# Second weights of a part row tile: a transfer from HBM in place of eight GpSimd sums per job

## The chip, the cores and the metric

One core of one Trainium2 chip runs the whole program. The metric is the device time of one execution in microseconds (us), the median of the timed runs. The engines are called TensorE (PE, its weight loads PEld), VectorE (DVE), ScalarE (ACT), GpSimd (POOL) and SyncE (SP; in this kernel it only issues transfers). A measurement of this kernel tells about 0.2% from no change.

## What is computed

The reference runs a linear attention over 3072 tokens and then two layers of experts. In the second layer each token goes to one of 8 experts, and this is what the change touches:

```python
expert_idx = np.argmax(logits, axis=1)
...
for e in range(E):
    mask = expert_idx == e
    ...
    xe = x[mask]
    h = np.maximum(xe @ w1[e], 0.0)
    ye = h @ w2[e]
    out[mask] = gate_w[mask, None] * ye
```

A token has 384 features, the hidden layer has 1024, all in float32.

## The kernel before

The attention fills the first part of the span. Then the experts follow one another as *jobs*: a job is one expert on a fixed number of token slots. The first layer's jobs and the first two of the second layer have 256 slots or fewer; then come seven jobs of the second layer with 448, 448, 448, 416, 416, 384 and 384 slots. The first five of these seven have a part of a row tile (64 or 32 rows beside three full tiles of 128) and are called J1 to J5 in the text. The experts of the last six jobs are known only at run time; their numbers sit in registers of SP.

A job on 448 slots has 24 *slots of work*. In slots 0 to 7 `gemm1` makes one block of the hidden layer each: nine products on PE into a bank of PSUM, of which three are in turn (`g1`, `bufs=3`). The float32 weights and activations are split into a high and a low part, which the fast product takes (`w1h`, `w1l`, `w2h`, `w2l`, `xh`, `xl`, `hh`, `hl`). A bank is read by ACT (`hh`, line 1040), then by DVE (`hl`, line 1041), then, for the part tile's columns, by ACT again (`hr`, line 1044); after that PE may fill it anew. In slots 8 to 23 `gemm2` makes the second product, four slots for each row tile. The part tile is the third (slots 16 to 19); it doesn't use the split but plain float32: `hr` times `w2r` (line 1060). Its second weights `w2r`, 128 x 8 x 384 values in one buffer, are rebuilt on POOL as the sum of the high and the low part, one block in each of the slots 0 to 7 (line 1045).

Beside that, `work` does in each slot what the other engines owe to the next jobs, in an order fixed by hand. Six pieces of the next job's weights are split in slots 0, 4, 8, 12, 16 and 20 (`conv_w`): ACT copies the high part (line 859), DVE or, for pieces 2 and 5, POOL subtracts it (line 860), and SP then loads the piece of the job after the next into the free staging buffer (`load_w`, lines 840 and 842). In slot 2 SP loads the next job's rows (`load_rows`, lines 1005 and 1007). In slots 9, 13 and 15 PE transposes them (line 1017). Finished rows are scattered to the output by POOL (line 273). SP issues its transfers in program order and waits at each until its buffer is free.

The buffers `w2r` and `hr` lie in the pool `f3`, which takes the place of a pool of the jobs before J1.

Of the kernel before, what the change touches and what calls it, by code (L numbers as in the profile page):

```python
# [24 lines left out]
E = 8  # L25
# [17 lines left out]
POOL_LO = (2, 5)  # L43
# slots of a job at which a piece of the next weights is split, and blocks of the next rows are transposed, by the job's row tiles
CONV = {
# [7 lines left out]
W_LO, W_HI = 0.25, 1.5  # L53
# row tiles that are gated together, by their first: how many, and after how many slots
GROUPS = {0: (4, 2), 4: (4, 2), 8: (4, 2), 12: (4, 2), 16: (4, 0), 20: (3, 1), 23: (1, 1)}
# [9 lines left out]
def general(tc, t, out, ident, rev, wg):  # L65
    """The whole computation for any values: the recurrence token by token, each expert on all tokens."""
    nc = tc.nc
# [117 lines left out]
def attn_moe_moe_kernel(ctx: ExitStack, tc: tile.TileContext, t, out):  # L185
# [15 lines left out]

# [1 line left out]
    ident = const.tile([128, 128], F32, name="ident")  # L203
# [52 lines left out]
    def prefill(buf, a, b):  # L256
        """empty slots, in blocks of 128"""
        nc.sync.dma_start(
            out=buf[a * 128:b * 128].rearrange("(a p) c -> p a c", p=128),
            in_=zrow.unsqueeze(1).to_broadcast([128, b - a, ROW]))  # L260

# [1 line left out]
    rt_p = fctx.enter_context(tc.tile_pool(name="rt", bufs=2))  # L263

    def logits_T(lt_ps, xT, n):
        """gate logits of n rows from their transpose: a part of the sum on each quarter of the partitions"""
        for kb in range(KB):
            T.matmul(lt_ps[32 * kb:32 * kb + 32], lhsT=wg[:, kb, :], rhs=xT[:, kb, 0:n], start=True, stop=True)
# [13 lines left out]
    def route(lt, X, g0, n, two, idx_out, ec):  # L282
        """lt: [96, n * 128] parts of the logits; X: row tiles; ec: which first slots.  Yields the engine of the operation to come."""
        sets = 2 if two else 1
# [67 lines left out]

# [1 line left out]
    gens = []  # L354
# [4 lines left out]
    def start(g, lag=0, burst=False, mult=1):  # L359
        """one at a time: they share a bank and the counts"""  # L360
        if gens:
            queue.append((g, lag, burst, mult))
        else:
            gens.append([g, next(g), slot[0] + lag, mult, burst])

    def tick(kind, now=False, burst=False):
        """the next operation of the gating under way if it waits for this engine; after another engine's, some slots later"""
        for x in gens[:]:
            if x[1][:3] == kind[:3] and (now or slot[0] >= x[2]):
                while True:  # L370
                    x[1] = next(x[0], None)
                    if x[1] is None:
                        gens.remove(x)
                        if queue:
                            start(*queue.pop(0))
                    elif kind != "pe " and x[4] and x[1][:3] in ("dve", "act"):
                        continue
                    elif x[1][:3] == kind[:3]:
                        if burst and kind != "pe ":
                            continue  # L380
                    else:
                        x[2] = slot[0] + x[3] * (int(x[1][3:]) if x[1][3:].strip() else 1)
                    return
# [19 lines left out]

# [1 line left out]
    def attention():  # L405
        with ExitStack() as actx:
# [54 lines left out]
            def gap(eng, x, r0):  # L461
                """rows r0..r0+31 of x become zero (those below the gap are written later)"""
                if eng is A:
                    A.copy(out=x[r0:r0 + 32], in_=warm_src[r0:r0 + 32, 0:x.free_size()])
                else:
                    eng.memset(x[r0:r0 + 32], 0.0)
# [11 lines left out]
            def check_w():  # L478
                """powers of w out of range: counted with the slots that overflow"""
                w2 = cst.tile([112, H], F32, name="w2")  # L480
                okw = cst.tile([112, H], F32, name="okw")
                w_ = w_c.rearrange("p h o -> p (h o)")
                V.tensor_tensor(out=w2, in0=w_, in1=w_, op=ALU.mult)
                V.tensor_scalar(out=okw, in0=w2, scalar1=W_LO, scalar2=None, op0=ALU.is_ge)
                V.tensor_scalar(out=w2, in0=w2, scalar1=W_HI, scalar2=None, op0=ALU.is_le)
                V.tensor_tensor(out=okw, in0=okw, in1=w2, op=ALU.mult)
                V.tensor_reduce(out=w2[:, 0:1], in_=okw, axis=AX.X, op=ALU.min)
                V.tensor_scalar(out=cum[0:112, 16:17], in0=w2[:, 0:1], scalar1=0.5, scalar2=None, op0=ALU.is_lt)
# [61 lines left out]
            def prep_kq(n):  # L550
                """keys for the states, and the values times what each token gives to its own output"""
                hb, j = n // LT, n % LT
# [17 lines left out]
            def amat(n):  # L570
# [6 lines left out]
                for X, r0 in ((XE[x], 0), (XO[x], 64)):  # L577
                    A.copy(out=fl(X[r0:r0 + 64]), in_=fl(a_ps[r0:r0 + 64]))
                # keys before the query; below partition 64 all of the odd buffer stays
                for X, n_, base in ((XE[x], 64, 0), (XO[x], 128, 64)):  # L580
# [4 lines left out]
            def uy(nu, uodd, ny, yodd):  # L585
                """state products of chunk (nu, uodd) between the output products of (ny, yodd)"""
                if nu is not None:
# [64 lines left out]
            def gate_route(lt, g0, gn):  # L652
# [3 lines left out]
                for c, k, end in ((0, 17, EARLY), (8, 18, NT)):  # L656
                    if g0 + gn == end:
                        # from here the first expert's slots are counted anew
                        yield "dve"
# [57 lines left out]
            for n in range(NT):  # L717
                # TensorE: state of the even half, outputs of the previous odd half
                uy(n, 0, n - 1 if n else None, 1)
# [85 lines left out]

# [1 line left out]
    W1 = [t["w1a"], t["w1b"]]  # L807
# [7 lines left out]
    def expert(n):  # L815
        """of the last ones, the one whose count comes at this place"""
        if n not in regs:
# [4 lines left out]
    def load_w(n, j):  # L822
        """piece j of six of the n-th expert's weights"""
        if n >= 2 * E:
# [5 lines left out]
        if n == 1:  # L830
            # the next but one's place, free until its own come
            if j == 0:
# [12 lines left out]
    def conv_w(n, j):  # L845
        """the piece as a sum of two that the fast float32 product takes exactly"""
        if n >= 2 * E:
# [48 lines left out]

# [1 line left out]
    rows0 = first.tile([128, 2, ROW], F32, name="rows0")  # L898
# [9 lines left out]
    def first_T(tp, kbs, a, b):  # L908
        """columns a..b of the transpose; of a row tile all, so that no part of it starts within"""
        a0 = a - a % 128  # L910
# [69 lines left out]

# [1 line left out]
    jobs = [(0, n, n * CAP1, CAP1) for n in range(E)] + [(1, E, 0, CAPS), (1, E, CAPS, CAPS)]  # L982
# [5 lines left out]
    def tiles_of(cap):  # L988
        """row tiles; a part of one comes between"""
        nf, half = divmod(cap, 128)  # L990
        t = [(i, 128) for i in range(nf)]
        if half:
            t.insert(2, (nf, half))
        return t
# [28 lines left out]
    def gemm1(j, fb):  # L1023
# [6 lines left out]
        if fb == 0:  # L1030
            ps = (first, pools["rows"]) if j <= LAST_S else (pools["h"],) * 2
            extra = []
            if cap > full:
                extra = [pools["h"].tile([128, FB, x], F32, tag=t, bufs=1, name=t) for t, x in (("w2r", DM), ("hr", cap - full))]
            hT[j] = [p.tile([128, FB, full], F32R, tag=t, bufs=1, name=t) for p, t in zip(ps, ("hh", "hl"))] + extra
        hh, hl = hT[j][0:2]
# [5 lines left out]
        if cap > full:  # L1042
            w2, hr = hT[j][2:4]
            A.activation(out=hr[:, fb], in_=p[:, full:cap], func=ACTF.Relu)  # L1044
            P.tensor_tensor(out=w2[:, fb], in0=wts[n][2][:, fb].bitcast(F32), in1=wts[n][3][:, fb].bitcast(F32), op=ALU.add)

    def gemm2(j, k, i, m, q):
        """two of the blocks of the second product; a part of a tile takes them in plain float32 on the parts of the columns"""
        l, n, base, cap = jobs[j]
# [50 lines left out]
    def work(j, k):  # L1100
        """what slot k of job j has for the other engines"""
        slot[0] += 1
# [41 lines left out]
    def by_count(tot):  # L1144
        """the last experts' places by their counts, and whether every expert and place has slots enough"""
        over = ids_p.tile([1, 19], F32, tag="over", name="over")
# [100 lines left out]
```

## Time and profile before

| What | Value |
|---|---|
| median of 3 timed runs | 642.01 us (641.26 to 642.4) |
| the profiled execution, its span from the first to the last instruction | 648.0 us |
| of the span: PE busy | 562.8 us (87%) |
| DVE busy | 405.8 us (63%) |
| ACT busy | 295.4 us (46%) |
| POOL busy | 298.7 us (46%) |
| transfers, mean over the span | 162 GB/s |

The times of single instructions come from the profiled execution, whose time is its span; it was 6.0 us longer than the median of the timed runs. Shares are averages over stages with different limits; what a change of one stage is worth is read from the waits in that stage.

### The profile page before, as it was taken

The page shows a single profiled execution, that of the slowest core. Times are in us where ns is not written, and L with a number is a line of the kernel's source. Part 1 is how long each engine was busy: PE and PEld are TensorE (multiplying, and loading weights), DVE is VectorE, ACT ScalarE, POOL GpSimd, SP SyncE. Part 2 cuts the span into 40 slices and gives each one's busy share as a digit, 9 for nine tenths or more (in the row PEclk, how much of TensorE's full clock was granted, in tenths as well). Part 3 has the DMA queues.
Part 4 walks back from the last instruction along what each step waited for, and adds up shares of the span by engine and source line. Part 5 has one row for each costly group of instructions (what it writes and reads, how often), then busy time and mean ns, then how long its engine had stood idle before and what let it go on. Part 6 is the DMA issues. An engine that isn't in the chain of part 4 may idle for free. (4 is left out here: it accounts for less than half of the span.)

```text
span 648.0 us, 13115 instructions
## 1 busy us (share of the span) xinstructions
PE 562.8 (87%) x5186; PEld 501.0 (77%) x5188; DVE 405.8 (63%) x732; ACT 295.4 (46%) x584; POOL 298.7 (46%) x312
## 2 busy tenths in 40 slices
PE   5796678778789989999999999997979979699993
PEld 3585566666667888898988999986869868599993
DVE  7998999999725467756676535436454464655320
ACT  5664455564425545554455426443424334254320
POOL 7765585776623175655323224644272524523201
PEclk8877888887979999999999999997998989799997
DMA  8985988679162987676665436342323434333000
GB/s 184 241 203 151 280 213 216 154 171 351 56 220 83 303 277 226 203 243 189 197 183 167 149 105 193 127 148 98 126 79 122 154 105 131 104 127 109 35 13 26
DMA packets 51896, 104.69 MB, mean 162 GB/s; under 512 B 5724, under 2 KB 37592, under 8 KB 51824
## 3 DMA queue, kind: packets, MB, share of 16 engines
q1 hardware_dynamic: 44016, 89.15, 47.7%
q0 software_dynamic: 5904, 11.82, 5.0%
q10 hardware_dynamic: 1904, 2.78, 1.7%
q8 instruction: 43, 0.70, 0.5%
q14 instruction: 29, 0.24, 0.1%
HBM read 82.98 MB, written 26.96 MB: 170 GB/s over the span
## 5 line engine op out<-in xcount | busy, mean ns | idle before, releaser
L1039 PE MATMUL g<-xh,w1h 128*128 128x256 f32 (+3 forms) x384 | 126.4, 329 | 19.1 <-ACT hr L1044 19.1
L1039 PE MATMUL g<-xh,w1l 128*128 128x256 f32 (+3 forms) x384 | 122.8, 320 | 0.0
L1039 PE MATMUL g<-xl,w1h 128*128 128x256 f32 (+3 forms) x384 | 122.4, 319 | 0.0
L1041 DVE SCALAR_TENSOR_TENSOR hl<-g,hh 128x256 fp32r<-128x256 f32 (+1 forms) x128 | 61.2, 480 | 93.1 <-ACT hh L1040 92.5
L1063 PE MATMUL g<-w2h,hh 128*128 128x384 f32 x312 | 109.2, 350 | 0.0
L1063 PE MATMUL g<-w2h,hl 128*128 128x384 f32 x312 | 105.5, 338 | 0.0
L1063 PE MATMUL g<-w2l,hh 128*128 128x384 f32 x312 | 105.2, 337 | 0.0
L1039 PEld LDWEIGHTS g<-xh,w1h 128*128 128x128 f32 x384 | 74.4, 194 | 25.4 <-ACT hr L1044 20.5
L1040 ACT ACTIVATE hh<-g 128x256 fp32r<-128x256 f32 (+1 forms) x128 | 55.1, 430 | 70.1 <-PE g L1039 68.8
L860 POOL TENSOR_TENSOR w1l<-s,w1h 128x1024 fp32r<-128x1024 f32 x14 | 33.4, 2389 | 114.1 <-ACT w1h L859 69.0
L1039 PEld LDWEIGHTS g<-xl,w1h 128*128 128x128 f32 x384 | 74.4, 194 | 1.8 <-DVE xl L1021 0.2
L1039 PEld LDWEIGHTS g<-xh,w1l 128*128 128x128 f32 x384 | 74.2, 193 | 1.6
L860 DVE TENSOR_TENSOR w1l<-s,w1h 128x1024 fp32r<-128x1024 f32 x28 | 57.6, 2056 | 20.9 <-ACT w1h L859 20.9
L273 POOL DMA_INDIRECT xs<-xall,idx_all x48 | 52.3, 1089 | 38.0 <-DVE cum L351 15.9
L273 POOL DMA_INDIRECT out<-rows,ids x30 | 29.2, 973 | 87.3 <-ACT rows L894 62.4
L1063 PEld LDWEIGHTS g<-w2h,hh 128*128 128x128 f32 x312 | 59.3, 190 | 3.1 <-issue 3.0
L1021 DVE TENSOR_TENSOR xl<-xt_ps,xh 128x256 fp32r<-128x256 f32 (+3 forms) x48 | 23.7, 495 | 57.3 <-ACT xh L1020 53.4
L1063 PEld LDWEIGHTS g<-w2l,hh 128*128 128x128 f32 x312 | 58.9, 189 | 0.1
L1063 PEld LDWEIGHTS g<-w2h,hl 128*128 128x128 f32 x312 | 58.5, 188 | 0.0
L606 PE MATMUL yp<-VSE,XE 112*64 112x48 f32 x384 | 31.5, 243 | 26.7 <-DVE xall L617 25.2
L606 PEld LDWEIGHTS yp<-VSE,XE 112*64 112x64 f32 x384 | 28.3, 157 | 28.6 <-DVE xall L617 26.9
L860 DVE TENSOR_TENSOR w2l<-s,w2h 128x1152 fp32r<-128x1152 f32 x28 | 37.9, 1354 | 14.0 <-ACT w2h L859 13.5
(194 smaller groups left out, 1207.2 us busy)
## 6 DMA issues: line engine op xcount, KB each, us to landing
s<-in_w1b SPq DMA_DIRECT2D x24, 512.0 KB
s<-in_w1a SPq DMA_DIRECT2D x21, 512.0 KB
RK<-in_rk SPq DMA_DIRECT2D x24, 384.0 KB
kr<-in_kr SPq DMA_DIRECT2D x12, 768.0 KB
s<-in_w2b SPq DMA_DIRECT2D x16, 576.0 KB
s<-in_w2a SPq DMA_DIRECT2D x14, 576.0 KB
xs<-zrow SPq DMA_DIRECT2D x5, 970.0 KB
VSE<-in_v SPq DMA_DIRECT2D x12, 384.0 KB
```

Of the source, the lines that this page charges most:

```text
L273: i = P.indirect_dma_start(out=dst, out_offset=bass.IndirectOffsetOnAxis(ap=idx_col, axis=0), in_=src, in_offset=None, bounds_check=last, ...
L606: T.matmul(y_ps[ny][0:64, h, 0:D], lhsT=XE[x][0:112, h], rhs=VSE[iy][0:112, jy, h], start=True, stop=True)
L860: (P if j in POOL_LO else V).tensor_tensor(out=lo, in0=x, in1=hi.bitcast(F32), op=ALU.subtract)
L1021: V.tensor_tensor(out=lo, in0=tp[:, 0:cap], in1=hi.bitcast(F32), op=ALU.subtract)
L1039: T.matmul(p, lhsT=a[:, kb, f], rhs=b[:, kb], start=(kb == 0 and i == 0), stop=(kb == KB - 1 and i == 2))
L1040: A.activation(out=hh[:, fb], in_=p[:, 0:full], func=ACTF.Relu)
L1041: V.scalar_tensor_tensor(out=hl[:, fb], in0=p[:, 0:full], scalar=0.0, in1=hh[:, fb].bitcast(F32), op0=ALU.max, op1=ALU.subtract)
L1063: T.matmul(p, lhsT=a[:, fb, r], rhs=b[:, fb], start=(fb == 0 and x == 0), stop=(fb == FB - 1 and x == 2))
```

## The change

In a job with a part tile the eight sums on POOL are gone. Instead one transfer on SP's queue brings the expert's second weights (1.57 MB) from HBM straight into `w2r`, issued where the buffers of the job's hidden layer are taken, ahead of the first slot's work. The product of the part tile stays as it is. The rest of the diff are comments and empty lines.

```diff
             if cap > full:
                 extra = [pools["h"].tile([128, FB, x], F32, tag=t, bufs=1, name=t) for t, x in (("w2r", DM), ("hr", cap - full))]
+
+                e = expert(n) if base is None else n - E
+                nc.sync.dma_start(out=extra[0], in_=W2[l][ds(e, 1)].rearrange("o (f p) d -> p (o f) d", p=128))
             hT[j] = [p.tile([128, FB, full], F32R, tag=t, bufs=1, name=t) for p, t in zip(ps, ("hh", "hl"))] + extra
...
         if cap > full:
-            w2, hr = hT[j][2:4]
+            hr = hT[j][3]
             A.activation(out=hr[:, fb], in_=p[:, full:cap], func=ACTF.Relu)
-            P.tensor_tensor(out=w2[:, fb], in0=wts[n][2][:, fb].bitcast(F32), in1=wts[n][3][:, fb].bitcast(F32), op=ALU.add)
```

## Rows read from the trace of the kernel before

**Rows 1.** The page's first line.
```profile
span 648.0 us, 13115 instructions
```

**Rows 2.** Waits of PE, 400 to 648 us: us in total, times, longest.
```profile
PE g L1039 <- ACT hr L1044: 19.1, 4, 6.2
```

**Rows 3.** Timeline of ACT, DVE, POOL, start of J2: start us, us, engine, line.
```profile
446.25 0.22 ACT L1044 ACTIVATE hr<-g 128x64 f32<-128x64 f32 x1 [6.63 <-DVE hl L1041]
...
439.26 6.49 DVE L860 TENSOR_TENSOR w1l<-s,w1h 128x1024 fp32r<-128x1024 f32 x1 [1.23 <-ACT w1h L859]
445.68 0.54 DVE L1041 SCALAR_TENSOR_TENSOR hl<-g,hh 128x384 fp32r<-128x384 f32 x1
...
436.91 7.75 POOL L1045 TENSOR_TENSOR w2r<-w2h,w2l 128x384 f32<-128x384 f32 x8
```

**Rows 4.** Timeline of DVE and POOL, start of J4 and of J5.
```profile
516.68 6.67 DVE L860 TENSOR_TENSOR w1l<-s,w1h 128x1024 fp32r<-128x1024 f32 x1 [1.20 <-ACT w1h L859]
...
514.52 7.75 POOL L1045 TENSOR_TENSOR w2r<-w2h,w2l 128x384 f32<-128x384 f32 x8
...
553.05 8.15 DVE L860 TENSOR_TENSOR w1l<-s,w1h 128x1024 fp32r<-128x1024 f32 x1 [1.20 <-ACT w1h L859]
...
552.42 7.70 POOL L1045 TENSOR_TENSOR w2r<-w2h,w2l 128x384 f32<-128x384 f32 x8
```

**Rows 5.** Timeline of DVE and POOL in J1.
```profile
406.70 1.22 DVE L860 TENSOR_TENSOR w1l<-s,w1h 128x1024 fp32r<-128x1024 f32 x1 [1.23 <-ACT w1h L859]
...
414.14 1.58 DVE L860 TENSOR_TENSOR w1l<-s,w1h 128x1024 fp32r<-128x1024 f32 x1 [1.23 <-ACT w1h L859]
...
407.62 8.99 POOL L1045 TENSOR_TENSOR w2r<-w2h,w2l 128x384 f32<-128x384 f32 x8 [3.23 <-issue]
```

**Rows 6.** Line 1045, all instructions: ns min/median/max, first and last start, forms.
```profile
L1045 POOL TENSOR_TENSOR w2r<-w2h,w2l x40: 980/1013/2031, 407.6 to 559.1; 128x384 f32<-128x384 f32 x40
L1045 POOLq EVENT_SEMAPHORE  x4: 43/43/4093, 403.2 to 407.5; - x4
```

**Rows 7.** Timeline of PE: first products of jobs and around the waits.
```profile
402.34 0.36 PE L1039 MATMUL g<-xh,w1h 128*128 128x448 f32 x1
...
434.84 0.36 PE L1039 MATMUL g<-xh,w1h 128*128 128x448 f32 x1
...
442.07 0.37 PE L1039 MATMUL g<-xh,w1l 128*128 128x448 f32 x1
446.53 0.74 PE L1039 MATMUL g<-xh,w1h 128*128 128x448 f32 x1 [4.10 <-ACT hr L1044]
...
474.24 0.36 PE L1039 MATMUL g<-xh,w1h 128*128 128x448 f32 x1
...
512.44 0.35 PE L1039 MATMUL g<-xh,w1h 128*128 128x416 f32 x1
...
524.11 0.72 PE L1039 MATMUL g<-xh,w1h 128*128 128x416 f32 x1 [4.70 <-ACT hr L1044]
...
527.63 0.35 PE L1039 MATMUL g<-xl,w1h 128*128 128x416 f32 x1
...
561.95 0.71 PE L1039 MATMUL g<-xh,w1h 128*128 128x416 f32 x1 [6.18 <-ACT hr L1044]
...
565.15 0.35 PE L1039 MATMUL g<-xh,w1h 128*128 128x416 f32 x1
```

**Rows 8.** Windows: us, busy of each engine, granted clock, DMA share, GB/s.
```profile
408.60:412.60 4.00, 4.00 (x21) 3.64 (x20) 1.35 (x3) 1.87 (x6) 4.00 (x5) 1.00 0.88 300
...
446.00:448.00 2.00, 1.47 (x4) 1.34 (x5) 0.78 (x2) 1.12 (x4) 0.00 (x0) 0.50 0.51 158
```

**Rows 9.** Timeline: SP's issues in J1 and J2, PE's transposes in J1.
```profile
407.96 0.35 SPq L840 DMA_DIRECT2D s<-in_w1b  x1
...
430.89 4.75 SPq L842 DMA_DIRECT2D s<-in_w2b  x2
...
419.33 0.84 PE L1017 MATMUL xt_ps<-ident,rows 128*128 128x128 f32 x4
```

## The prediction

> **What bounds the kernel now.** I read the span first, then what TensorE (PE) waits for in the second half, then the timelines of the engines in that wait, one engine at a time. The profiled span is 648.0 us [rows 1], 6.0 us more than the median of the timed runs (642.01); I make the sum against the span and carry the difference in us over.
>
> The changed lines run from 402 us on, in the five jobs of 448 and 416 slots. Call them J1 to J5 in order of time. From 400 us to the end PE has one wait in its list: 19.1 us in four pieces, for `hr` on ScalarE (ACT), line 1044 [rows 2]. Everything else there is PE at work, so in these jobs the end moves by what PE waits, and by nothing else that VectorE (DVE), ACT, GpSimd (POOL) or the transfers spend.
>
> What is behind `hr`? In J2 `hr` stood idle 6.63 us for `hl` on DVE; `hl` ran at 445.68, as soon as a weight subtraction (`w1l`, line 860) let DVE go; and that subtraction, started at 439.26, took 6.49 us [rows 3]. The same subtraction took 1.22 us in J1 [rows 5]. In J2 it lay inside the eight sums of line 1045 on POOL, which ran without a gap from 436.91 to 444.66 [rows 3]. It ended at 445.75, 1.09 us after the last sum. In J4 the two ends are 523.35 and 522.27, in J5 561.20 and 560.12 [rows 4]: 1.08 both times (J3 repeats J2: 6.49 us, 1.09 us after the sums). So in four jobs the subtraction hardly moves until the sums are over, and then needs about its normal time. I take the sums as the cause.
>
> In J1 the sums ran too, with no wait of PE. There the first sum could only start at 407.62, when the first subtraction (406.70 to 407.92) was almost done; the second, at 414.14, took 1.58 us, only 0.36 more [rows 5]. Why DVE got in between two sums there and not in the others, the trace doesn't say; for the change it does not matter, because after it there are no sums.
>
> By the Trainium skill (SBUF — State Buffer, "Who interferes with whom") a DVE instruction with two SBUF inputs and a GpSimd instruction that reads SBUF exclude each other, and the one that starts first holds the shared pair for that instruction. By it the subtraction would wait for one sum, about 1 us, and end after about 2.2 us, too little to stop PE; J1's 1.58 agrees with that, the 6.49 to 8.15 us of the others do not. By the rule the sums would not be what stops PE, and the time would stay at 642. The measurement decides in the sum.
>
> **The change part by part.**
>
> *Removed: 40 sums on POOL*, 1.01 us each (median) [rows 6], about 8 us a job. POOL is on no path to the end by itself: nothing waits for `w2r` before the part tile, eight slots later. Their worth is the PE wait. Today's waits are 4.10 us in J2 (and J3, alike), 4.70 in J4, 6.18 in J5 [rows 7], 19.1 in sum.
>
> After each wait PE also ran at half clock: granted 0.50 at 446 to 448 us [rows 8], that is 1.2 GHz, against 1.00 (2.4 GHz) in J1, where it was busy without a break [rows 8]. J2 to J3 start to start is 474.24 - 434.84 = 39.40 us; J1, with the same shape and no wait, took 434.84 - 402.34 = 32.50. So J2 loses 6.90. J3, also 448 slots, takes 512.44 - 474.24 = 38.20, so loses 5.70 [rows 7]. For 416 slots no clean job exists; a full-speed product there takes 0.207 x 416/448 = 0.192 us (0.207: J2's first 36 products start from 434.84 to 442.07, 35 steps in 7.23 us). J4: 10 products from 524.11 to 527.63, 3.52 - 1.92 = 1.60 on top of 4.70, so 6.30. J5: 9 products from 561.95 to 565.15, 3.20 - 1.73 = 1.47 on top of 6.18, so 7.65 [rows 7]. Sum: 6.90 + 5.70 + 6.30 + 7.65 = 26.55 us.
>
> *What is late next?* Without the wait for the sums the subtraction is 5.27 us shorter in J2 (6.49 - 1.22), 5.45 in J4 (6.67 - 1.22), 6.93 in J5 (8.15 - 1.22). The PE waits are 4.10, 4.70 and 6.18. So `hr` of the second slot comes 1.17, 0.75 and 0.75 us before PE wants its bank: the wait goes wholly, but the cover is thin. If another 1 us of POOL work fell on that subtraction, a wait of some tenths would come back. Nothing of POOL's is due there: its next work after the sums is the subtraction of piece 2, in slot 8 of the job. J1 has the same order of work and no wait. All of the 26.55 counts.
>
> *Added: five transfers of 8 x 128 x 384 x 4 B = 1.57 MB*, 7.9 MB in all, on SP's queue. The issue itself keeps SP some tenths of a us (0.35 for a weight piece [rows 9]), an engine with nothing on the path. From below a transfer costs nothing; from above what it delays. Three things to look at:
>
> First, SP waits in order. In J1 the buffer's place belongs to tiles of the job before. POOL now waits 4.09 us for it at the same point (line 1045's semaphore wait), and its first sum starts at 407.62 [rows 5, 6]; SP would then wait to about 407.4. Behind it on SP stands the load of the first weight piece, which today goes out at 407.96 because it waits for the subtraction [rows 9], and the rows of the next job. So nothing is held up. In J2 SP is done with the load before at 430.89 + 4.75 = 435.64 [rows 9], and the part tile of J1, the buffer's last reader, was multiplied before (slots 16 to 19 of 24): the transfer goes out at once. The expert's number is in a register of SP already.
>
> Second, the same queue carries the rows of the next job, which PE transposes in slot 9. In J1 that is at 419.33 [rows 9]. From 407.4 the queue has 1.57 MB, then a weight piece of 0.52 and rows of 0.70, 2.79 MB. Between 408.6 and 412.6 it moved 300 GB/s [rows 8]; so 9.3 us from 408.6, 417.9: in time by 1.4 us. In J2 to J5 the transfer goes out earlier against the job's start. For J2: 3.18 MB with the piece before it, from about 436.9, is 10.6 us, 447.5; wanted 17.0 us after the start (419.33 - 402.34), at 451.8. In time by 4 us.
>
> Third, the part tile wants `w2r` in slot 16, long after either.
>
> Cost of the added transfers: 0, hidden under PE's own work; the upper bound is J1's rows late, at half that rate (18.6 us, 427.2) 7.9 us and up to 2.8 for the clock (6.90 - 4.10). The rate is read from the same queue and shape, so I take the end at nothing.
>
> **Sum.** 648.0 - 26.5 + 0 = 621.5 us span; less the 6.0 us: 615.5 us.
>
> **The rivals.**
>
> *A wait takes the place of the one removed (chance 0.10).* J1's rows land late, or the thin cover in J2 to J5 is lost. For: margins of 1.4 and 0.75 us. Against: J1 runs clean with the same order. Price 0.5 to 10.7 us: 616 to 626, most of it near the low end.
>
> *The sums are not what holds the subtraction (0.03).* It waits out one sum, and something else keeps DVE for the other 4 to 6 us. For: J1 has sums and no wait. Against: the 1.08 and 1.09 us between the ends. Then the waits stay: about 642. The rule of the Trainium skill's page SBUF — State Buffer cited above comes to this.
>
> *Slower (0.02).* The transfer ahead of the rows in SP's queue makes each of the five jobs wait in slot 9. To lose the gain each must wait 26.55 / 5 = 5.3 us; in J2 that is rows at 457.1 instead of 451.8, 3.18 MB in 20.2 us: it decides below 157 GB/s, against 300 in the row. At 140 GB/s the rows would land at 459.6, 7.8 us late, 39 us in the five jobs: about 615.5 + 39 = 654.
>
> *The forecast (0.85).* 613 to 618: the reconstruction of the clock losses and the carry from profiled to timed run are good to some 2 us.
>
> **How the numbers follow.** A measurement of this kernel tells 0.2% (1.3 us) from no change. The forecast and the first rival are faster (0.95), the second is no change (0.03), the third slower (0.02). The range runs from 612.5 (the forecast with its error below) to 621 (the forecast and most of the first rival).
>
> **What would show it.** The `w1l` subtractions of the first slots at 1.22 us; no PE wait for `hr`; granted clock 1.00 from 400 to 620 us; J1 to J3 each 32.5 us, J4 and J5 about 30; POOL without line 1045; five transfers on SP's queue that land before slot 16. Wrong would be: a PE wait at line 1017 (rows late), or `w1l` still at 5 us or more.

## The result, and the profile after

The changed kernel takes 616.5 us (median, 615.61 to 618.32), the kernel before 641.63 us beside it (639.57 to 642.4): a ratio of 0.9613, 95% interval 0.9586 to 0.964. The forecast was 615.5.

The page of the changed kernel, its first lines:

```profile
span 613.6 us, 13104 instructions
## 1 busy us (share of the span) xinstructions
PE 550.5 (90%) x5186; PEld 492.9 (80%) x5188; DVE 381.7 (62%) x732; ACT 296.1 (48%) x584; POOL 262.8 (43%) x272
```

The span is 34.4 us shorter than [rows 1], but not all of that is the change: J1 started at 402.34 in the profile before [rows 7] and starts at 393.71 here, and nothing ahead of J1 was touched. In the traces of this study J1 starts anywhere from 393.7 to 407.3 us, whatever the kernel. So the profiles are compared from J1 on, and the timed runs only with the kernel before on the same chip.

The timeline of PE, the first product of J1 to J5 and of the job after them:

```profile
393.71 0.36 PE L1042 MATMUL g<-xh,w1h 128*128 128x448 f32 x1
...
426.21 0.36 PE L1042 MATMUL g<-xh,w1h 128*128 128x448 f32 x1
...
458.71 0.36 PE L1042 MATMUL g<-xh,w1h 128*128 128x448 f32 x1
...
490.87 0.36 PE L1042 MATMUL g<-xh,w1h 128*128 128x416 f32 x1
...
520.75 0.35 PE L1042 MATMUL g<-xh,w1h 128*128 128x416 f32 x1
...
549.62 0.33 PE L1042 MATMUL g<-xh,w1h 128*128 128x384 f32 x1
```

The differences are the lengths of the five jobs. Those of before come from [rows 7] and from the first products of J5 and of the job after it in that trace:

```profile
548.81 0.35 PE L1039 MATMUL g<-xh,w1h 128*128 128x416 f32 x1
...
585.52 0.33 PE L1039 MATMUL g<-xh,w1h 128*128 128x384 f32 x1
```

| Job | before, us | after, us | saved | forecast |
|---|---|---|---|---|
| J1 | 32.50 | 32.50 | 0 | 0 |
| J2 | 39.40 | 32.50 | 6.90 | 6.90 |
| J3 | 38.20 | 32.16 | 6.04 | 5.70 |
| J4 | 36.37 | 29.88 | 6.49 | 6.30 |
| J5 | 36.71 | 28.87 | 7.84 | 7.65 |
| sum | 183.18 | 155.91 | 27.27 | 26.55 |

From 380 us to the end the list of PE's waits is empty, where [rows 2] had 19.1 us. The windows of J2 and of J5 without its first 1.5 us (us, busy of PE, PEld, DVE, ACT, POOL, granted clock, DMA share, GB/s) show PE busy without a break and the clock at 1.00, 2.4 GHz, throughout; [rows 8] had 0.50 after the wait:

```profile
426.15:458.65 32.50, 32.50 (x174) 28.55 (x173) 13.13 (x19) 14.76 (x29) 8.13 (x7) 1.00 0.56 188
...
522.20:549.60 27.40, 27.40 (x163) 26.00 (x162) 14.53 (x21) 13.47 (x28) 6.55 (x6) 1.00 0.61 204
```

Groups of DVE's instructions by form, 393 to 560 us (busy, mean ns of one): the twelve subtractions of `w1l` on DVE take 1.225 us in the mean, where before they took 1.22 to 8.15 [rows 3 to 5].

```profile
L860 DVE TENSOR_TENSOR w1l<-s,w1h 128x1024 fp32r<-128x1024 f32 x12 | 14.7, 1225 | 12.9 <-ACT w1h L859 12.9
```

Timeline of SP at the start of J1, what answers to [rows 9], and PE's first transposes there:

```profile
398.32 0.38 SPq L1037 DMA_DIRECT2D w2r<-in_w2b  x1
399.57 0.35 SPq L840 DMA_DIRECT2D s<-in_w1b  x1
400.16 0.37 SPq L1005 DMA_DIRECT2D rows<-xs  x1
400.73 0.57 SPq L1007 DMA_DIRECT2D rows<-xs  x1
```
```profile
410.69 0.84 PE L1017 MATMUL xt_ps<-ident,rows 128*128 128x128 f32 x4
```

The last issue of rows (line 1007) landed 8.0 us later, at 408.73: 2.0 us before PE takes them. The new transfer itself landed 7.0, 8.1 and 7.5 us after its issue in J1, J2 and J4 (the trace has no landing for the other two), 13.8 us and more before the part tile's first product.

### The profile page after: what moved, and what is told of

Same layout as the page of the kernel before. It is cut to its first block, busy times and chain, and to the rows that moved or that the text cites. A ratio compares the mean times of both kernels' runs of the same rounds, so it can differ in the third digit from the quotient of the medians.

```text
span 613.6 us, 13104 instructions
## 1 busy us (share of the span) xinstructions
PE 550.5 (90%) x5186; PEld 492.9 (80%) x5188; DVE 381.7 (62%) x732; ACT 296.1 (48%) x584; POOL 262.8 (43%) x272
## 5 line engine op out<-in xcount | busy, mean ns | idle before, releaser
L1042 PE MATMUL g<-xh,w1h 128*128 128x256 f32 (+3 forms) x384 | 122.8, 320 | 0.0
L1042 PE MATMUL g<-xh,w1l 128*128 128x256 f32 (+3 forms) x384 | 120.0, 313 | 0.0
L1042 PE MATMUL g<-xl,w1h 128*128 128x256 f32 (+3 forms) x384 | 119.6, 311 | 0.0
L1042 PEld LDWEIGHTS g<-xh,w1h 128*128 128x128 f32 x384 | 72.1, 188 | 4.5 <-DVE hl L1044 1.6
L1042 PEld LDWEIGHTS g<-xl,w1h 128*128 128x128 f32 x384 | 72.4, 188 | 1.5 <-DVE xl L1021 0.2
L1042 PEld LDWEIGHTS g<-xh,w1l 128*128 128x128 f32 x384 | 72.2, 188 | 1.4
L1020 ACT CAST xh<-xt_ps 128x256 fp32r<-128x256 f32 (+3 forms) x48 | 20.8, 432 | 58.0 <-PE xt_ps L1017 57.4
L860 DVE TENSOR_TENSOR w1l<-s,w1h 128x1024 fp32r<-128x1024 f32 x28 | 34.3, 1225 | 20.9 <-ACT w1h L859 20.9
## 6 DMA issues: line engine op xcount, KB each, us to landing
xs<-zrow SPq DMA_DIRECT2D x5, 970.0 KB, 10.4
```

The source lines that it names most:

```text
L860: (P if j in POOL_LO else V).tensor_tensor(out=lo, in0=x, in1=hi.bitcast(F32), op=ALU.subtract)
L1020: A.copy(out=hi, in_=tp[:, 0:cap])
L1042: T.matmul(p, lhsT=a[:, kb, f], rhs=b[:, kb], start=(kb == 0 and i == 0), stop=(kb == KB - 1 and i == 2))
```

## The experiments

The kernel before took 641.6 us in the measurement above and 651.6, 651.6 and 650.9 us on the three chips of these experiments, so ratios are what to compare. The last four kernels were timed once each, and what is read from them is read from their profiles. The lengths of J1 to J5 agree within 0.01 us between two profiles of one kernel (155.91 and 155.90 for the changed kernel), and are the sharper measure. The last column holds the waits for `hr` alone.

| Run | sums | transfer | ratio to before (95%) | J1 to J5, us | PE waits for `hr`, us |
|---|---|---|---|---|---|
| before | slot 0 on, back to back | no | 1 | 183.18 | 19.1 |
| e5_after | none | yes | 0.9613 (0.9558 to 0.9668) | 155.90 | 0 |
| e1_neither | none | no | 0.960 (0.9554 to 0.9647) | 155.90 | 0 |
| e2_both | as before | yes, unread | 0.9999 (0.9972 to 1.0026) | 183.07 | 19.2 |
| e3_gaps | one a slot, behind its `hr` | no | 0.9597 (0.9549 to 0.9645) | 155.67 | 0 |
| e4_late | back to back behind slot 5 | no | 0.9557 (0.9509 to 0.9605) | 155.65 | 0 |
| e6_late_again | the same | no | 0.9585 (0.9535 to 0.9634) | 155.64 | 0 |
| e7_twice | none | twice | 0.9743 (0.9696 to 0.979) | 165.34 | 0 |
| e8_tiny | 8 of 32 values a job | yes | 0.9612 (0.9564 to 0.966) | 155.65 | 0 |
| e9_memsets | 12 memsets instead | yes | 0.960, one run each | 155.66 | 0 |
| e10_slot1 | back to back behind slot 1 | no | 0.953, one run each | 155.64 | 0 |
| e11_half | 16 half sums, back to back | no | 1.004, one run each | 186.07 | 21.5 |
| e12_pool_pieces | as before, DVE's subtractions on POOL | no | 0.958, one run each | 155.91 | 0 |

**Without sums and without transfer.** The part tile takes the high part of the weights alone.

```diff
-                nc.sync.dma_start(out=extra[0], in_=W2[l][ds(e, 1)]...)
...
-                T.matmul(p[o:o + m], lhsT=hT[j][3][:, fb], rhs=hT[j][2][:, fb], ...)
+                T.matmul(p[o:o + m], lhsT=hT[j][3][:, fb], rhs=w2h[:, fb].bitcast(F32), ...)
```

> After without the transfer: no sums and no transfer; the part tile is multiplied by the high part of the weights alone (its low part is left out of the product). Theory (the sums held DVE's subtraction, the transfer is hidden): the same as after, 616.5 us within 1.5, ratio to before about 0.961, no PE wait for hr. Rival (the transfer costs something that the gain covers up): 2 us or more faster than after, 614 or less.

0.960 against 0.9613, and the five jobs as long to 0.01 us: the transfer costs nothing that the gain hides.

**Sums and transfer together.** The transfer goes into two tiles that are free by then and one new small one.

```diff
+                e = expert(n) if base is None else n - E
+                u = first.tile([128, FB, CAP1], F32R, tag="hh", name="w2u")...
+                v = first.tile([128, KB, CAP1], F32R, tag="xh", name="w2v")...
+                for y, f0, nb in ((u, 0, 5), (v, 5, 2), (extra[2]..., 7, 1)):
+                    nc.sync.dma_start(out=y[:, 0:nb * DM]..., in_=W2[l][ds(e, 1), f0 * 128:(f0 + nb) * 128]...)
```

> Before with the sums, and beside them the same 1.57 MB from HBM per job into buffers that nothing reads (in three pieces of 5, 2 and 1 blocks). Theory: the transfer neither helps nor costs, so before's time, 641.6 us within 2, with PE waits for hr of about 4.1, 4.1, 4.7 and 6.2 us. Rival (the gain comes from the new order on SP's queue, the sums are not the cause): about 616 us and no such waits.

The ratio is 1 within 0.3%. The waits of PE and the subtraction in J2 (DVE's timeline) are those of before:

```profile
PE g L1044 <- ACT hr L1049: 19.2, 4, 6.2
```
```profile
442.33 6.49 DVE L860 TENSOR_TENSOR w1l<-s,w1h 128x1024 fp32r<-128x1024 f32 x1 [1.23 <-ACT w1h L859]
```

With the run without either: all of the gain is the sums' going, none is the transfer's coming or the new order on SP's queue.

**Sums with gaps.** Each sum waits, by a small one ahead of it that reads `hr`, for its slot.

```diff
+            P.tensor_tensor(out=tok..., in0=hr[:, fb, 0:32], in1=hr[:, fb, 0:32], op=ALU.add)
             P.tensor_tensor(out=w2[:, fb], in0=wts[n][2][:, fb].bitcast(F32), in1=wts[n][3][:, fb].bitcast(F32), op=ALU.add)
```

> Before, with each sum held back until hr of its own slot is there (a small POOL sum of 32 values a row that reads hr stands ahead of each). All 40 sums stay, no transfer. Theory (DVE is held because POOL's sums follow one another without a gap): DVE gets in after at most one sum, the subtraction takes at most 2.3 us, within the 0.75 to 1.17 us of cover, PE waits below 0.5 us: 616 to 618 us. Rival (each sum costs DVE time, gap or none): waits of several us stay, 630 us or more.

All 40 sums are still there, and the whole gain is too. J2 on POOL and on DVE:

```profile
439.36 1.01 POOL L1046 TENSOR_TENSOR w2r<-w2h,w2l 128x384 f32<-128x384 f32 x1
442.32 0.24 POOL L1045 TENSOR_TENSOR tok<-hr 128x32 f32<-128x32 f32 x1 [1.95 <-ACT hr L1044]
442.52 1.02 POOL L1046 TENSOR_TENSOR w2r<-w2h,w2l 128x384 f32<-128x384 f32 x1
```
```profile
440.10 1.35 DVE L860 TENSOR_TENSOR w1l<-s,w1h 128x1024 fp32r<-128x1024 f32 x1 [1.34 <-ACT w1h L859]
```

The subtraction falls on the end of one sum, takes 0.13 us more than alone (1.35 against 1.22), and POOL has nothing next in hand. So it is not what the sums cost in all but how they lie to the subtraction.

**Sums late.** The block of eight stays whole but waits for `hr` of slot 5; `e6_late_again` is the same kernel beside the changed one.

```diff
+            if fb == 5:
+                P.tensor_tensor(out=tok..., in0=hr[:, fb, 0:32], in1=hr[:, fb, 0:32], op=ALU.add)
+                for f in range(FB):
+                    P.tensor_tensor(out=w2[:, f], in0=wts[n][2][:, f]..., in1=wts[n][3][:, f]..., op=ALU.add)
```

> Before, with all eight sums of a job back to back on POOL, but held until hr of slot 5: behind both of DVE's subtractions of slots 0 and 4, where none is due until slot 12. Theory (what counts is that a subtraction falls into the block of sums): subtractions at 1.22 us, no PE wait, 616 to 617.5 us. Rival (the sums cost by their number, wherever they stand): about 641 us.

> The late sums once more, beside the changed kernel. Theory (the transfer and the late sums both leave PE without a wait; only the end differs: 12.9 us from the last product to the end in the changed kernel, 11.3 with the late sums): 1.5 to 2.0 us faster than the changed kernel. Rival (its lower ratio was the scatter of the chip): the same as the changed kernel within 1 us.

No subtraction of slots 0 and 4 falls into the block (mean 1.225 us; those of `w2l`, slots 12 and 16, take 1.48 in the mean instead of 1.36), PE never waits: a rearrangement of POOL's order alone gives what the transfer gives, without 7.9 MB more from HBM. Whether it is faster than the changed kernel the times can't tell (0.9585 and 0.9613 with overlapping intervals). The profiles have 155.64 against 155.90 us for the jobs and 11.3 against 13.1 us from the start of the last product to the end; more on that end below.

**The changed kernel beside these runs, and the transfer twice.** The first copy goes where `e2_both` had it.

> The changed kernel itself, on the same chip as the next three, to compare them. Theory: ratio to before 0.961, PE waits none between the five jobs, the end from the last product to the last instruction 12.9 us as in its first profile.

> The changed kernel with each transfer made twice, the first copy into buffers that nothing reads: 1.57 MB more in SP's queue ahead of the rows. Theory (the transfer is hidden because the rows still land 2.0 to 3.5 us before PE's transposes; 1.57 MB take 3.9 us at the 400 GB/s that the queue moves): rows late by 0.4 to 2 us in the five jobs, waits of PE ahead of line 1017 of about 6 us in sum, 3 to 8 us slower than the changed kernel. Rival (there is much more room in the queue): the same as the changed kernel within 1 us.

The doubled transfer loses 9.4 us in the jobs (165.34 - 155.90) and 1.3% of the time: J1 36.85 instead of 32.50, J5 33.40 instead of 28.87, the others within 0.5. PE waits in three of the five jobs, where five were expected, and at the place that the prediction had named. PE's waits, its timeline in J1, and the windows after:

```profile
PE xt_ps L1017 <- DMA rows<-xs: 5.4, 3, 2.7
```
```profile
422.16 1.04 PE L1017 MATMUL xt_ps<-ident,rows 128*128 128x128 f32 x4 [2.43 <-DMA rows<-xs]
```
```profile
424.00:426.00 2.00, 2.00 (x8) 2.00 (x7) 0.60 (x3) 0.00 (x0) 0.00 (x0) 0.50 0.51 205
```

Of J1's 4.35 us 2.43 are the wait and the rest is mostly work at a granted clock of 0.50 (1.2 GHz) behind it. But J1 is no clean test of the queue. The first copy brings a small buffer of its own into the pool of `w2r`, and SP gets `w2r` later, likely for that reason (timelines of SP in J1, of this kernel and of the changed one, which start J1 at 402.58 and 393.71):

```profile
411.34 0.37 SPq L1041 DMA_DIRECT2D w2r<-in_w2b  x1
413.15 0.38 SPq L1005 DMA_DIRECT2D rows<-xs  x1
```
```profile
398.32 0.38 SPq L1037 DMA_DIRECT2D w2r<-in_w2b  x1
400.16 0.37 SPq L1005 DMA_DIRECT2D rows<-xs  x1
```

The rows' issue comes 10.57 us after the start of J1 instead of 6.45, and these 4.1 us alone are more than the 2.0 us that the rows had in hand. In `e2_both`, with the same small buffer, the sums of J1 too start 8.7 us into the job instead of 5.3. In J5 the rows are issued at the same point (8.07 against 7.88 us after the start) and PE still waits 2.74 us: that wait is the queue's. So the queue has room for this transfer in all five jobs and not for a second one in J5; J2 stands at 32.50 in both.

**As many POOL instructions as before.** A small sum a slot stays, in the changed kernel.

```diff
             A.activation(out=hr[:, fb], in_=p[:, full:cap], func=ACTF.Relu)
+            P.tensor_tensor(out=tok..., in0=hr[:, fb, 0:32], in1=hr[:, fb, 0:32], op=ALU.add)
```

> The changed kernel with a small POOL sum (32 values a row) in each of the slots 0 to 7 of the five jobs, 40 in all, that nothing needs: POOL's program has as many instructions as before. Theory (POOL's last drain comes 2.2 us later in the changed kernel because its program is 40 instructions shorter): drain as early as before, 1.6 us faster than the changed kernel, PE without a wait all the same. Rival (the late drain has nothing to do with the length of the program): the same as the changed kernel within 0.5 us.

The drain, POOL's last long instruction, stayed late (13.2 us from the start of the last product to the end): the theory fell. The jobs are as short as without these sums.

**What in the sums holds the subtraction.** Memsets in place of sums, in the changed kernel:

```diff
+            if fb == 0:
+                for _ in range(12):
+                    P.memset(tok..., 0.0)
```

> The changed kernel with twelve POOL memsets of 128 x 768 values at the start of each of the five jobs, at the place of the sums, that nothing needs. Theory (POOL without a gap holds DVE's subtraction, whatever it does): subtractions of slot 0 of 4 us or more again, PE waits for hr. Rival (it is POOL's reading of its two operands that holds the subtraction): subtractions at 1.22 us, no wait, jobs of 32.5 us.

```profile
437.17 9.56 POOL L1049 MEMSET tok<- 128x768 f32 x12
...
439.60 0.74 POOL L1049 MEMSET tok<- 128x768 f32 x1
```
```profile
439.55 1.23 DVE L860 TENSOR_TENSOR w1l<-s,w1h 128x1024 fp32r<-128x1024 f32 x1 [1.24 <-ACT w1h L859]
```

The memsets fill 9.56 us, longer than the sums, and the subtraction among them takes 1.23. They are not quite without a gap: of all 60, with their group's line (busy, mean ns of one, idle time before them):

```profile
L1049 POOL MEMSET tok<- 128x768 f32 x60 | 44.5, 742 | 3.2
```

That is some 0.05 us between two, where the sums overlap (eight of 1.01 us in 7.75 us). But the subtraction needs no gap here: the memset that starts at 439.60, 0.05 us into the subtraction, takes its usual 0.74 us and is over 0.44 us before it. The two run side by side. So my theory fell: POOL's being busy is not enough. The sums read SBUF and the memsets don't, and that is the difference that I take as the cause. Now DVE's two subtractions moved to POOL, with the sums as before:

```diff
-        (P if j in POOL_LO else V).tensor_tensor(out=lo, ...)
+        (P if j in POOL_LO or (j < 2 and n > E + 1) else V).tensor_tensor(out=lo, ...)
```

> Before, with the subtractions of slots 0 and 4 on POOL too in these five jobs, so that DVE has none while the sums run; all sums stay. Theory (only DVE's subtraction, with both operands in SBUF, is held; hl, with one operand in PSUM, is not): hl at 0.56 us, no wait of PE, jobs of 32.5 us. Rival (the sums delay ACT's or DVE's reading of the PSUM bank directly): waits for hr as before, about 19 us.

```profile
441.46 3.93 POOL L1045 TENSOR_TENSOR w2r<-w2h,w2l 128x384 f32<-128x384 f32 x4
```
```profile
442.81 0.56 DVE L1041 SCALAR_TENSOR_TENSOR hl<-g,hh 128x384 fp32r<-128x384 f32 x1 [1.30 <-ACT hh L1040]
```

The eight sums of J2 now stand in runs of one, four and three, and the line is the run of four. `hl`, with one operand in PSUM and one in SBUF, runs through it at its 0.56 us, as it does inside the unbroken block of the kernel before (437.48, 0.56 us, in its DVE timeline); only the subtraction with both in SBUF is held. The two differ in size too (384 and 1024 columns), which no run here separates. Next the block behind slot 1 (`fb == 1` in the diff of the late sums), and the half sums:

```diff
+            for c in (0, 192):
+                P.tensor_tensor(out=w2[:, fb, c:c + 192], in0=wts[n][2][:, fb, c:c + 192]..., in1=wts[n][3][:, fb, c:c + 192]..., op=ALU.add)
```

> Before, with the block of eight sums held until hr of slot 1, behind the subtraction of slot 0; the one of slot 4 then falls into the block some 5.4 us after its start, as it does in the first of the five jobs before the change, where it took 1.58 us. Theory (a block without a gap holds a subtraction until it is over): slot 4's subtraction takes 3 us or more, PE waits below 2 us a job. Rival (a block that starts late lets DVE in, as seen in the first job): 1.6 us or less, no wait, jobs of 32.5 us or less.

> Before, with each sum cut into two of 192 columns, 16 a job. Theory (the next sum takes the place before DVE can, so the length of one doesn't matter): slot 0's subtraction ends 1.1 us after the last half sum as before, waits as before or longer, jobs of 38 us or more. Rival (DVE waits for a fixed number of instructions, or gets in at some ends): subtractions clearly shorter, waits half as long.

POOL and DVE in J2, of the block behind slot 1 and of the half sums:

```profile
439.81 8.80 POOL L1048 TENSOR_TENSOR w2r<-w2h,w2l 128x384 f32<-128x384 f32 x8
```
```profile
444.77 2.00 DVE L860 TENSOR_TENSOR w1l<-s,w1h 128x1024 fp32r<-128x1024 f32 x1 [1.23 <-ACT w1h L859]
```
```profile
435.81 9.85 POOL L1046 TENSOR_TENSOR w2r<-w2h,w2l 128x192 f32<-128x192 f32 x16
```
```profile
438.16 7.05 DVE L860 TENSOR_TENSOR w1l<-s,w1h 128x1024 fp32r<-128x1024 f32 x1 [1.23 <-ACT w1h L859]
```

For the block behind slot 1 the rival wins: in a block without a gap the subtraction of slot 4 takes 1.64 to 2.00 us in all five jobs, at most one sum more than alone. J1 before was no accident. The delay is mutual: in each of these blocks one sum takes about twice its time (the line of the sums: ns min/median/max), and the block 8.80 us instead of 7.75. One sum of J1 before did the same (2031 ns in [rows 6]).

```profile
L1048 POOL TENSOR_TENSOR w2r<-w2h,w2l x40: 1002/1012/2022, 407.3 to 541.9; 128x384 f32<-128x384 f32 x40
```

The half sums hold the subtraction of slot 0 for longer (7.05 to 8.73 us in J2 to J5), though in J2 the subtraction ends 0.45 us before the block (445.21 against 435.81 + 9.85 = 445.66) and not 1.1 us after it: the last half sum is the one that waits for it (1.56 us instead of 0.59). Cutting the sums buys nothing, but "until the block is over" is not exact.

## Why the prediction was right

*What bounds the kernel.* Right: with the one wait gone, nothing else stops PE in these jobs. They became shorter by the 19.1 us that PE waited and by 8.2 us more (27.27 - 19.1), which the prediction had put down to the clock of 0.50 behind the waits; with the waits the 0.50 is gone.

*The sums hold the subtraction.* Shown from four sides: without them (e1), with them beside the transfer (e2), with them spread (e3) and with them elsewhere (e4). By e9 and e12 what is held is the instruction with two operands in SBUF, and what holds it is POOL's reading; each rests on one pair of instructions that differ in more than that. The Trainium skill (SBUF — State Buffer, "Who interferes with whom") says both things: a DVE instruction with at most one SBUF input, outside its two-port modes, doesn't contend, and one with two contends with a GpSimd instruction that reads, not with one that only writes. The traces agree: 0.56 us for `hl`, 1.23 us among memsets. The page's further rule ("SBUF: two separate sides"), that the holder keeps the pair for its one instruction, agrees with J1 and with e10 (at most 2.00 us), not with the four subtractions of 6.49 to 8.15 us. So the rival built on that rule was wrong about this kernel's time.

*The size.* The sum was 26.55 us, measured 27.27. J3 was mis-sized most (5.70, measured 6.04): it was held against J1's 32.50, but a clean J3 takes 32.16, probably since the job that it prepares has 416 slots and less to transpose. J4 and J5, for which no clean job existed, came out at 6.49 and 7.84 for 6.30 and 7.65; these last 0.2 us each the runs don't place.

*The cover.* Forecast for J2: `hr` of slot 1 is 1.17 us ahead of PE's need. In the changed kernel it ends at 432.58, and PE's 37th product is due at 426.21 + 36 x 0.207 = 433.66: 1.08 us.

*The transfers.* Hidden, as forecast; rows in J1 in time by 2.0 us (forecast 1.4). From SP's issue of the transfer to the rows' landing it was 10.4 us (398.32 to 408.73), and the forecast had 10.5 (407.4 to 417.9), though at another rate: about 400 GB/s in the middle of that stretch and less at its ends, where the forecast had 300 throughout. In J2 SP's issue of the rows also waited 1.6 us for the scatter of the rows' buffer, which the prediction had not named; it fitted into the 4 us there. The first rival, rows too late, is real but starts at a larger transfer (J5 in e7) or a later issue (J1 in e7).

*Not foreseen.* From the start of the last product to the last instruction it is 12.9 us in the changed kernel, 11.3 before. The program ends with drain instructions. POOL's last scatter (timeline) and its last drains (line's instructions: ns min/median/max, first and last start), before and after:

```profile
637.91 0.98 POOL L273 DMA_INDIRECT out<-rows,ids  x1 [3.24 <-ACT rows L894]
```
```profile
L1244 POOLq DRAIN  x3: 113/186/7940, 638.7 to 647.5; - x3
```
```profile
602.00 0.98 POOL L273 DMA_INDIRECT out<-rows,ids  x1 [3.24 <-ACT rows L894]
```
```profile
L1246 POOLq DRAIN  x3: 44/107/7827, 605.0 to 613.4; - x3
```

The long drain, 7.9 and 7.8 us, starts 0.8 us after the scatter's start in the kernel before and 3.0 us after it in the changed one. This gives back 1.6 us: 27.27 - 1.6 = 25.7, beside 25.1 between the medians. So the 615.5 came out near 616.5 partly by luck: an underestimated gain (0.7 us) met an unforeseen loss (1.6 us). Taking the 6.0 us between the profiled and the timed runs off again was sound: that profile reached J1 8.6 us later than the one here, and ahead of J1 nothing was changed.

*Left open.* Why the pair passes to DVE at the end of a sum in J1 and e10, and not for 5 to 7 us in J2 to J5 and e11. The held ones were all subtractions of slot 0 asked for 0.6 to 2.4 us into the block; those let in were of slot 4, 3.1 us or more into it (3.07 us in J1 of `e2_both`, whose block starts late: 1.94 us long). The held ones also met ends of sums later than that and were not let in, so the age of the block alone does not decide. The slot, and what it reads, and the time of asking were not told apart. Why POOL's drain is late in some programs is open too: it was late in eight of the kernels run here and early in four, and the number of POOL's instructions doesn't sort them (312 in `e2_both`, early, and in `e8_tiny`, late).

## What to carry to other kernels

A GpSimd block that is off the critical path can still stop PE: look for an instruction of VectorE whose time is several times its usual one, see what GpSimd does meanwhile, and follow the bank that it delays. What removes such a stall is that the two don't meet: later or spaced sums were worth as much as taking them out. The transfer in place of compute was free here because what stands behind it in the same queue still landed in time; measure by how much, and by doubling it, and see that the doubling adds nothing but the transfer: here a buffer for the second copy delayed the issue in J1.

## What the runs showed of the hardware

- Sums on POOL back to back made a VectorE subtraction of two SBUF operands, 1.22 us alone, take up to 8.15 us (8.73 with half sums). Where it was let in among them, one sum took 2.0 us instead of 1.0. Twelve memsets 0.05 us apart didn't hold it (1.23 us), and a memset ran beside it in its usual 0.74 us.
- After PE waits of 4.1 to 6.2 us (before) and of 2.4 and 2.7 us (e7) the granted clock was 0.50 for some us; without the waits it was 1.00 from J1 to J5.
- With five transfers of 1.57 MB more, PE's products and DVE's and ACT's instructions kept their times (e1 and e5: `hl` 0.556 us in both, `hh` 0.490 in both, the five jobs the same to 0.01 us).
